# Batch 2 of a fused forgetting attention and GELU network: all AV heads behind the last scores, and the first GEMM opened with seven blocks

## The chip, the cores and the metric

The kernel runs on one core of a Trainium2 chip. The metric is device time in microseconds (us) of one execution, lower is better. The kernel before took 330.33 us, the median of three runs (329.3 to 330.56).

## What is computed

Attention with a decay per key and a causal mask, for 8 batches of 8 heads, 576 tokens and head size 64, followed by a network of two matrix products with an exact GELU between them, on 4608 tokens:

```python
scores = scale * q @ k.T                       # per batch and head, scale = 1 / sqrt(64)
cum = cumsum(log(clip(f, 1e-4, 1)))
scores = where(causal, -1e9, scores + cum[:, None] - cum[None, :])
attn = softmax(scores)
x = (attn @ v) with heads side by side         # 4608 x 512
h = x @ w_in                                   # 512 x 2048
out = (0.5 * h * (1 + erf(h / sqrt(2)))) @ w_out   # 2048 x 512
```

## The kernel before

All inputs of the matrix products are bf16, all sums are float32 in PSUM. The decay is put into v: `weigh_v` (line 283) multiplies v of each key by its weight and adds the weight itself as a 65th column, so that one product gives the numerator and the denominator of the softmax. It runs on GpSimd (POOL in the profile).

**Names.** Heads go in pairs, `i` = 0 to 3. `scores(b, i, t)` (line 299) writes one of four tiles of K x Q products of a pair into PSUM (two matmuls of 64 rows side by side, one per head), ScalarE (ACT) takes the exponential into the tile `e`, and GpSimd zeroes what the mask forbids. `attend` (line 343) is the AV product of one head: for each of five blocks of 128 queries it runs over the keys up to the block, 15 matmuls of 128 x 65. `normalize` and `divide` (lines 358, 367) divide by the 65th column on VectorE (DVE) and leave x in bf16. `x_dma` (line 394) transposes x of a pair into `xT` by a DMA transpose from the SP queue. `tail` (line 401) is another way for the last 64 queries of a batch: `blocks` (line 364) then leaves the fifth block out of `attend`, and 40 matmuls with 64 columns give these queries for all heads, followed by a DMA transpose into `tails`. Where `attend` does all five blocks, `x_tail` (line 427) copies the last 64 columns of `xT` into `tails` on GpSimd. `av_both` (line 853) does both heads of a pair into one PSUM tile with one reciprocal and one divide.

**First GEMM.** `gemm1` (line 436) makes one of 16 blocks of 128 hidden units for the 512 first tokens of a batch: four matmuls of 128x512, one per pair `i` (so the matmul `kt` needs the `xT` of pair `kt`), then GELU on ScalarE into `g`. `gemm1_open` (line 873) begins seven blocks at once and goes through them pair by pair. The 64 last queries of each of the eight batches go through one more GEMM at the very end.

**Second GEMM.** It lags: `gemm2_rows(c, plan)` (line 524) is a generator that gives one step at a time, 16 steps for each group of 128 tokens. A step "n" is one matmul over 128 rows; a step "r" is two matmuls of 64 rows into two PSUM banks, which run side by side, as those of `scores` do. A group with "r" steps takes two evictions on VectorE, a copy and an add. `take(fill, n)` (line 625) puts n such steps behind a tile of scores, so TensorE (PE) has work while ScalarE takes the exponential. Batch 2 has more of them than the later ones, 112 (`gemm2_third`, line 620: 16 steps left over from batch 0, 32 more of batch 0, 64 of batch 1), while batches 3 to 7 have 64.

**Order.** The schedule is written out by hand. `attention(b)` (line 893) serves batches 2 to 7, in one way for batch 2 and in another for the later ones. In batch 2 the AV product of pair i - 1 comes after the second score tile of pair i, and that of the last pair after the last tile. In batches 3 to 7 the AV products of all pairs come behind the last tile of scores, then the tails, the rest of the GEMM2 steps and `gemm1_open`.

**SP queue.** One engine, SP, issues in program order and waits for each transfer's data before it issues the next: the v loads of the next batch (`load_v`, line 129, five transfers), the DMA transposes of its q and k (`transpose_dma`, line 245, heads 0 to 3 and 4 to 7), the stores of the output, and the x transposes. Loads of q and k (`load_qk_tokens`, line 98) go from GpSimd's queue. The transposed q and k are put in order by 32 copies on VectorE (`untangle`, line 260) during the first GEMM of the batch before.

PSUM has eight banks: the tiles "s" (two of two banks; scores, `av_both`, tails, GEMM1), "o" and "m" (two of one bank each; AV, GEMM1, GEMM2).

Of the kernel before, what the change touches and what calls it, by code (L numbers as in the profile page):

```python
# [9 lines left out]
FP32 = mybir.dt.float32  # L10
# [5 lines left out]
P = 128  # L16
# [3 lines left out]
HP = 4  # L20
NBLK = 5
# [33 lines left out]
def kernel(  # L55
# [10 lines left out]
    nc = tc.nc  # L66
# [62 lines left out]
    def load_v(b, h0=0, h1=H, eng=nc.sync, ns=range(NBLK)):  # L129
        if b >= B:  # L130
            return
        for n in ns:
            p0 = D if n == NBLK - 1 else 0
            eng.dma_start(
                v_sb[p0:P, h0:h1, n, :],
                v[b, h0:h1, K0[n] + p0 : K0[n] + P].rearrange("h p d -> p h d"),
            )
# [107 lines left out]
    def transpose_dma(b, h0, h1):  # L245

        if b >= B:
            return
        if b not in tq_of:
            tq_of[b] = [  # L250
                tq_pool.tile([P, H, JT // 2, PT], BF16, tag="t" + n, name=f"t{n}{b}")
                for n in "qk"
            ]
        for src, dst in zip(qk_of[b], tq_of[b]):
            nc.sync.dma_start_transpose(
                dst[:, h0:h1].rearrange("d h j p -> d (h j) p"),
                src[:, h0:h1].rearrange("p h c -> p (h c)"),
            )
# [103 lines left out]
        divide(x_of[b, i][:, 0:nm, h, :], o_of[b, i, h], nm)  # L362

    def blocks(b):
        return NBLK - 1 if b > 2 else NBLK

    def divide(x, o, n):
        r = x_pool.tile([P, NBLK], FP32, tag="r", name="r")
# [101 lines left out]
    def gemm2(c):  # L470
# [40 lines left out]
        (3, "m", 5 * "r" + 11 * "n"),  # L511
    ]

    PLAN_0 = [(2, "o", 16 * "r"), (3, "m", 14 * "r" + 2 * "n")]
    PLAN_1 = [
        (0, "m", 14 * "r" + 2 * "n"),
        (1, "m", 14 * "r" + 2 * "n"),
        (2, "m", 12 * "r" + 4 * "n"),
        (3, "s", 16 * "n"),
    ]  # L520

    put_off = []

    def gemm2_rows(c, plan):

        for ts, held, steps in plan:
            if held == "s":  # L530
                both = s_psum.tile([P, 2, d_model], FP32, tag="s", name="ps2")
                banks = [both[:, 0], both[:, 1]]
            else:
                pool = {"o": o_psum, "m": m_psum}[held]
                banks = [
                    pool.tile([P, d_model], FP32, tag=held, name="ps2")
                    for _ in range(2)
                ]
            ot = o_pool.tile([P, d_model], FP32, tag="ot", name="ot")
            for kt, step in enumerate(steps):  # L540
                last = kt == steps.rfind("r")
                for r in range(2 if step == "r" else 1):
                    rows = slice(r * D, (r + 1) * D) if step == "r" else slice(0, P)
                    nc.tensor.matmul(  # L544
                        banks[r],
                        g_of[c][kt][rows, ts * P : (ts + 1) * P],
                        w_out_sb[rows, kt, :],
                        start=kt == (steps.index("r") if r else 0),
                        stop=last if r else kt == n_ff - 1,
                    )  # L550
                if plan is PLAN and last and kt == n_ff - 1:
                    banks.reverse()
                if "r" in steps and (kt == n_ff - 1 if held == "s" else last):
                    copy = partial(nc.vector.tensor_copy, ot, banks[1])
                    if plan is PLAN and ts == 3:
                        put_off.append(copy)
                    else:
                        copy()  # L558
                if kt == n_ff - 1:
                    if "r" in steps:  # L560
                        sum_out(c, ts, ot, banks[0])
                    else:
                        nc.vector.tensor_copy(ot, banks[0])
                        store(c, ts, ot)
# [55 lines left out]
    def gemm2_third():  # L620
        yield from gemm2_second(0)
        yield from gemm2_rows(0, PLAN_0)
        yield from gemm2_rows(1, PLAN_1)

    def take(gen, n):
        for _ in range(n):
            if next(gen, "end") == "end":
                return
# [219 lines left out]


    FILL = [[8, 4, 3, 3], [3, 3, 3, 3], [3, 3, 3, 3], [3, 3, 3, 2]]  # L850
    FILL_2 = [[8, 8, 8, 8], [8, 8, 4, 4], [4, 4, 4, 4], [4, 4, 4, 4]]

    def av_both(b, i):

# [38 lines left out]
    def attention(b):  # L893


        fill = gemm2_third() if b == 2 else gemm2_rows(b - 1, PLAN)
        counts = FILL_2 if b == 2 else FILL

        def av(i, n=0):
            for h in range(2):  # L900
                attend(b, i, h, range(blocks(b)))
                normalize(b, i, h)
                if h == 0:
                    take(fill, n)
            x_dma(b, i)

        for i in range(HP):
            for t in range(4):
                scores(b, i, t)
                take(fill, counts[i][t])  # L910
                if t == 1 and b == 2 and i > 0:
                    av(i - 1)
                    if i == 1:
                        load_v(3)
                if b == 2 and (i, t) == (0, 3):
                    weigh_v(b, 2)
                    weigh_v(b, 3)
                if b > 2 and i == 0 and t == 1:
                    load_v(b + 1)
                if b > 2 and t == 0 and i < 2:  # L920
                    transpose_dma(b + 1, 4 * i, 4 * i + 4)
                if b == 2 and t == 1 and i == 1:
                    transpose_dma(3, 0, 4)
        if b == 2:
            take(fill, 4)
            av(HP - 1)
        else:
# [12 lines left out]
        if b == 2:  # L940
            pss = [gemm1(b, ffb, (0, 1)) for ffb in range(2)]
            pss += [spare(), spare()]
            for ffb in range(2):
                gemm1(b, ffb, (2,), pss[ffb])
            for ffb in (2, 3):
                gemm1(b, ffb, (0, 1, 2), pss[ffb])
            for ffb in range(4):
                gemm1(b, ffb, (3,), pss[ffb])
            more = s_psum.tile([P, 2, 512], FP32, tag="s", name="ps1")
            gemm1(b, 4, ps=more[:, 0, :])  # L950
        else:
# [70 lines left out]
    for b in range(B):  # L1022
        if b == 0:
            first_attention()
        elif b == 1:
            second_attention()
        else:
            attention(b)
        for ffb in range(4 if b < 2 else 5, n_ff):
            if b == 0 and ffb in HELD:  # L1030
                continue
            aside = ffb in ((7, 8) if b == 2 else (8, 9, 12, 13)) if b > 1 else b == 1 and ffb % 4 < 2
            if b <= 2 or ffb > 6:
                gemm1(b, ffb, ps=spare() if aside else None)
            if b == 1 and ffb % 2 == 0:
                at = HELD[(ffb - 4) // 2]
                gelu(0, at, h_of[at])
            if b == 0:
                if ffb == 4:
                    attend_tail()  # L1040
                if ffb == 5:
                    tail_0()
                if ffb == 7:
                    weigh_v(1, 0)
                    load_w_out(0)
                    weigh_v(1, 1)
                    load_w_out(1)
                    load_qk_tokens(2)
                if ffb == 8:
                    transposes_first(1, 0, o_psum, "o")  # L1050
            elif b + 1 < B:
                first, gap = (5, 3) if b == 1 else (1, 4)
                at, late = divmod(ffb - first, gap)
                if late == 0:
                    untangle(b + 1, at)
                if late == gap - 2 and (b > 1 or at < 2):
                    weigh_v(b + 1, at)
                if ffb == (9 if b == 1 else 14):
                    load_qk_tokens(b + 2)
# [34 lines left out]
```

## Time and profile before

| what | us |
|---|---|
| median of three runs | 330.33 |
| the profiled execution | 330.52 |
| its span, first to last instruction | 328.8 |
| TensorE busy | 318.2 (97%) |
| ScalarE, VectorE, GpSimd busy | 203.3, 180.5, 131.5 |
| batch 2: first score tile to first GEMM | 67.66 to 99.21 |
| batch 2: first GEMM | 99.21 to 113.11 |
| batch 3: the same two | 113.11 to 133.38, to 147.37 |
| batch 4: the same two | 147.37 to 167.40, to 181.37 |
| granted TensorE clock, mean | 0.998 |

Times in the profile count from the start of the span. PE is TensorE, PEld its weight loads, DVE VectorE, ACT ScalarE, POOL GpSimd, SP the engine that issues most DMAs. L440 is line 440 of the kernel: L319 are score matmuls, L350 and L412 AV and tails, L440 the first GEMM, L544, L608 and L584 the second, L396 the x transposes, L255 those of q and k, L134 the v loads, L572 stores. A few matmul records are missing from the trace, and busy times of overlapping matmuls are counted once.

### The profile page before, as it was taken

Reading aid. Unit: us, or ns where it says so; the run is one execution under the profiler, and the core shown is the slowest. Engines: PE = TensorE matmul, PEld = TensorE weight load, DVE = VectorE, ACT = ScalarE, POOL = GpSimd, SP = SyncE. Lnnn points to the kernel's source line nnn. Section 1 sums busy time; section 2 is a strip of 40 time slices with the busy share of each in tenths; the row PEclk is TensorE's granted clock in tenths of the full one; section 3 lists DMA queues with packets and bytes.
Section 4 is the critical chain, followed back from the end, with each engine's and each line's share of the span. In section 5 each row is a group of like instructions: output and inputs, shape, how many; then the busy total and the mean of one; then the engine's idle time right before and its main releaser. Section 6 shows DMA issues by size and latency. Waiting matters only on the chain.

```text
span 328.8 us, 8087 instructions
## 1 busy us (share of the span) xinstructions
PE 318.2 (97%) x3295; PEld 169.9 (52%) x3327; DVE 180.5 (55%) x422; ACT 203.3 (62%) x296; POOL 131.5 (40%) x255
## 2 busy tenths in 40 slices
PE   8899899999999999999999999999999999999995
PEld 4664546445554456445644565455645564444443
DVE  5952666684459935892599349953895270010011
ACT  4886776984635796189808990899178926405600
POOL 8996983029427053804471356225512500000000
PEclk9999999999999999999999999999999999999999
DMA  7999999979998899489959893969410131020013
GB/s 115 189 194 221 208 189 134 183 154 166 203 210 179 125 203 198 84 148 167 220 78 174 159 216 83 175 128 223 101 41 3 66 82 56 0 94 36 0 46 85
DMA packets 93829, 43.87 MB, mean 133 GB/s; under 512 B 73056, under 2 KB 88672, under 8 KB 93792
## 3 DMA queue, kind: packets, MB, share of 16 engines
q1 hardware_dynamic: 76640, 26.83, 40.7%
q0 software_dynamic: 16752, 15.99, 30.7%
q8 instruction: 26, 0.43, 0.6%
q10 hardware_dynamic: 400, 0.52, 0.4%
q14 instruction: 11, 0.09, 0.1%
HBM read 36.85 MB, written 9.44 MB: 141 GB/s over the span
## 4 chain that ended last, share of the span: by engine, by line
PE 86%; DMA 8%; POOL 3%; issue 1%; ACT 0%; DVE 0%; another core or an unknown queue 0%; POOLq 0%
PE ps L440 35%; PE ps L544 27%; PE ps L484 8%; PE o L350 6%; PE s L319 6%; DMA q<-in_k_dram 3%; DMA k<-in_k_dram 3%; DMA v_sb<-in_v_dram 2%; PE o L412 1%; PE ps L608 1%; POOL q L120 1%; PE ps L584 1%; POOL k L120 1%; POOL w_in_sb L184 1%; POOL vw L288 1%
## 5 line engine op out<-in xcount | busy, mean ns | idle before, releaser
L460 ACT ACTIVATE g<-ps 128x512 bf16<-128x512 f32 x138 | 75.8, 618 | 84.7 <-PE ps L440 83.5
L440 PE MATMUL ps<-xT,w_in_sb 128*128 128x512 bf16 x499 | 113.0, 379 | 1.5 <-DVE xT L706 0.3
L544 PE MATMUL ps<-w_out_sb,g 64*128 64x512 bf16 (+1 forms) x737 | 104.4, 376 | 0.8 <-issue 0.5
L329 ACT ACTIVATE e<-s 128x896 bf16<-128x896 f32 x112 | 87.8, 837 | 15.1 <-PE s L319 13.7
L440 PEld LDWEIGHTS <-w_in_sb 128*128 128x128 bf16 x576 | 55.2, 98 | 66.7 <-issue 2.6
L331 POOL TENSOR_SCALAR_AFFINE_SELECT e<-e 128x256 bf16<-128x256 bf16 (+1 forms) x135 | 49.1, 383 | 89.5 <-ACT e L329 89.1
L544 PEld LDWEIGHTS <-g 64*128 64x128 bf16 (+1 forms) x751 | 42.1, 94 | 31.3 <-issue 1.3
L288 POOL TENSOR_TENSOR vw<-v_sb,wT 128x640 bf16<-128x640 f32 (+1 forms) x30 | 38.0, 1270 | 31.6 <-DMA v_sb<-in_v_dram 15.8
L269 DVE COPY qT<-tq 64x288 bf16<-64x288 bf16 x96 | 43.6, 454 | 1.5
L558 DVE COPY ot<-ps 128x512 f32<-128x512 f32 x20 | 13.8, 692 | 54.3 <-PE ps L544 54.3
L319 PE MATMUL s<-qT,kT 64*128 64x256 bf16 (+1 forms) x336 | 37.8, 275 | 0.8 <-DVE kT L241 0.6
L269 DVE COPY kT<-tk 64x288 bf16<-64x288 bf16 x96 | 35.2, 367 | 5.3 <-DMA tk<-k 3.6
L493 DVE COPY ot<-ps 128x512 f32<-128x512 f32 (+2 forms) x9 | 5.7, 632 | 49.5 <-PE ps L484 49.5
L319 PEld LDWEIGHTS <-kT 64*128 64x128 bf16 x336 | 18.0, 94 | 19.8 <-issue 4.4
L484 PE MATMUL ps<-w_out_sb,g 128*128 128x512 bf16 (+2 forms) x142 | 27.9, 355 | 0.1
L370 DVE TENSOR_TENSOR x<-o,r 128x256 bf16<-128x256 f32 (+1 forms) x50 | 22.3, 446 | 4.3 <-DMA xT<-x 2.7
L350 PEld LDWEIGHTS <-e 128*128 128x128 bf16 x640 | 21.5, 98 | 4.3 <-issue 2.4
L350 PE MATMUL o<-vw,e 128*128 128x65 bf16 x640 | 22.6, 194 | 0.0
L484 PEld LDWEIGHTS <-g 128*128 128x128 bf16 x144 | 13.5, 98 | 14.5
L568 DVE TENSOR_TENSOR ot<-ot,ps 128x512 f32<-128x512 f32 x27 | 18.6, 688 | 3.0 <-remote 0.7
L440 PE MATMUL ps<-tails,w_in_sb 128*128 128x512 bf16 x64 | 14.3, 378 | 0.0
L369 DVE RECIPROCAL r<-o 128x4 f32<-128x4 f32 (+1 forms) x50 | 8.9, 179 | 8.1 <-PE o L350 3.9
(92 smaller groups left out, 195.1 us busy)
## 6 DMA issues: line engine op xcount, KB each, us to landing
out_dram<-ot SPq DMA_DIRECT2D x32, 256.0 KB, 2.6
v_sb<-in_v_dram SPq DMA_DIRECT2D x24, 256.0 KB, 5.0
q<-in_q_dram POOLq DMA_DIRECT2D x6, 576.0 KB, 7.0
k<-in_k_dram POOLq DMA_DIRECT2D x6, 576.0 KB, 9.7
v_sb<-in_v_dram POOLq DMA_DIRECT2D x17, 128.0 KB, 6.4
w_in_sb<-in_moe_w_in_dram POOLq DMA_DIRECT2D x4, 512.0 KB, 8.2
w_out_sb<-in_moe_w_out_dram POOLq DMA_DIRECT2D x4, 512.0 KB, 8.3
v_sb<-in_v_dram SPq DMA_DIRECT2D x6, 128.0 KB, 4.5
```

Source lines behind the costliest of these rows:

```text
L269: nc.vector.tensor_copy(rows[:, odd], src[odd * D : (odd + 1) * D, 2 * i + h].rearrange("d j p -> d p j"),)
L288: eng.tensor_tensor(vw(b)[:, hs, n0:n1, 0:D], v_sb[:, hs, n0:n1, :], w.unsqueeze(3).to_broadcast([P, 2, n1 - n0, D]), Alu.mult,)
L319: nc.tensor.matmul(to, *ab, start=half < 0, stop=half == 1 or not masked)
L329: nc.scalar.activation(et[:, :, z:c], st[:, :, z:c], Act.Exp, scale=scale)
L331: nc.gpsimd.affine_select(out=et[:, :, c0 + z : c0 + P], in_=et[:, :, c0 + z : c0 + P], compare_op=Alu.is_ge, fill=0.0, base=z, pattern=[[ ...
L350: nc.tensor.matmul(o[:, m, :], e_of[b, i, t][:, h, c : c + P], vw_of[b][:, 2 * i + h, n, :], start=(n == 0), stop=(n == m),)
L370: nc.vector.tensor_tensor(x, o[:, 0:n, 0:D], r[:, 0:n].unsqueeze(2).to_broadcast([P, n, D]), Alu.mult,)
L440: nc.tensor.matmul(ps, w_in_sb[:, kt, ffb * P : (ffb + 1) * P], xT(c)[:, kt, 0:TC] if c < B else tails[:, kt % 2, :, kt // 2, :], start=(k ...
L460: nc.scalar.activation(g_of[c][ffb], ps, Act.Gelu)
L484: nc.tensor.matmul(pss[ts][:, c0:c1], g_of[c][kt][:, ts * P : (ts + 1) * P], w_out_sb[:, kt, c0:c1], start=(kt == 0), stop=(kt == n_ff - 1),)
L544: nc.tensor.matmul(banks[r], g_of[c][kt][rows, ts * P : (ts + 1) * P], w_out_sb[rows, kt, :], start=kt == (steps.index("r") if r else 0), ...
L568: nc.vector.tensor_tensor(ot, ot, bank, Alu.add)
```

## The change

Batch 2 is given the order of batches 3 to 7. Its `attend` does four blocks, and `tail` the last 64 queries; its AV products all stand behind its last tile of scores; its first GEMM is opened by `gemm1_open`. GEMM2 of batch 1 uses the plan of the later batches (only the last group ends in "n" steps), and that of batch 0 only "r" steps. The steps behind each tile are dealt out anew (101 instead of 88 within the scores). The v loads of batch 3 and the first two transposes of its q and k stay behind the second tile of pair 1; the other two, which stood behind the last AV product, come behind the second tile of pair 2. Blocks 5 and 6 of the first GEMM are no longer made in the loop at the end of the file, since the opening makes them.

```diff
     def blocks(b):
-        return NBLK - 1 if b > 2 else NBLK
+        return NBLK - 1 if b > 1 else NBLK
...
-    PLAN_0 = [(2, "o", 16 * "r"), (3, "m", 14 * "r" + 2 * "n")]
-    PLAN_1 = [
-        (0, "m", 14 * "r" + 2 * "n"),
-        (1, "m", 14 * "r" + 2 * "n"),
-        (2, "m", 12 * "r" + 4 * "n"),
-        (3, "s", 16 * "n"),
-    ]
+    PLAN_0 = [(2, "o", 16 * "r"), (3, "m", 16 * "r")]
...
         yield from gemm2_rows(0, PLAN_0)
-        yield from gemm2_rows(1, PLAN_1)
+        yield from gemm2_rows(1, PLAN)
...
-    FILL_2 = [[8, 8, 8, 8], [8, 8, 4, 4], [4, 4, 4, 4], [4, 4, 4, 4]]
+    FILL_2 = [[8, 8, 8, 8], [8, 8, 8, 7], [5, 5, 5, 5], [5, 5, 6, 2]]
...
         for i in range(HP):
             for t in range(4):
                 scores(b, i, t)
                 take(fill, counts[i][t])
-                if t == 1 and b == 2 and i > 0:
-                    av(i - 1)
-                    if i == 1:
-                        load_v(3)
                 if b == 2 and (i, t) == (0, 3):
                     weigh_v(b, 2)
                     weigh_v(b, 3)
-                if b > 2 and i == 0 and t == 1:
+                if (i, t) == ((1, 1) if b == 2 else (0, 1)):
                     load_v(b + 1)
-                if b > 2 and t == 0 and i < 2:
-                    transpose_dma(b + 1, 4 * i, 4 * i + 4)
-                if b == 2 and t == 1 and i == 1:
-                    transpose_dma(3, 0, 4)
-        if b == 2:
-            take(fill, 4)
-            av(HP - 1)
-        else:
-            av(0)
-            av_both(b, 1)
-            av_both(b, 2)
-            av(3)
-            take(fill, 4)
-            tail(b)
-            put_off.pop()()
-        if b == 2:
-            take(fill, 4)
-            transpose_dma(3, 4, 8)
+                for half, at in enumerate([(1, 1), (2, 1)] if b == 2 else [(0, 0), (1, 0)]):
+                    if (i, t) == at:
+                        transpose_dma(b + 1, 4 * half, 4 * half + 4)
+        av(0)
+        av_both(b, 1)
+        av_both(b, 2)
+        av(3)
+        take(fill, 4)
+        tail(b)
+        put_off.pop()()
         take(fill, 999)
-
-        if b == 2:
-            pss = [gemm1(b, ffb, (0, 1)) for ffb in range(2)]
-            pss += [spare(), spare()]
...
-        else:
-            gemm1_open(b)
+        gemm1_open(b)
         if b + 1 < B:
             untangle(b + 1, 0)
             weigh_v(b + 1, 0)
-        if b == 2:
-            x_tail(b)
...
-            aside = ffb in ((7, 8) if b == 2 else (8, 9, 12, 13)) if b > 1 else b == 1 and ffb % 4 < 2
-            if b <= 2 or ffb > 6:
+            aside = ffb in (8, 9, 12, 13) if b > 1 else b == 1 and ffb % 4 < 2
+            if b < 2 or ffb > 6:
                 gemm1(b, ffb, ps=spare() if aside else None)
```

More of the change, by code (lines that the diff above doesn't have):

```diff
@@ L529, in gemm2_rows @@
         for ts, held, steps in plan:
-            if held == "s":
-                both = s_psum.tile([P, 2, d_model], FP32, tag="s", name="ps2")
-                banks = [both[:, 0], both[:, 1]]
-            else:
[L534 to L538, printed above, removed]
+            pool = {"o": o_psum, "m": m_psum}[held]
+            banks = [
+                pool.tile([P, d_model], FP32, tag=held, name="ps2") for _ in range(2)
+            ]
             ot = o_pool.tile([P, d_model], FP32, tag="ot", name="ot")
@@ L547, in gemm2_rows @@
                         w_out_sb[rows, kt, :],
-                        start=kt == (steps.index("r") if r else 0),
+                        start=kt == 0,
                         stop=last if r else kt == n_ff - 1,
@@ L552, in gemm2_rows @@
                     banks.reverse()
-                if "r" in steps and (kt == n_ff - 1 if held == "s" else last):
+                if last:
                     copy = partial(nc.vector.tensor_copy, ot, banks[1])
@@ L559, in gemm2_rows @@
                 if kt == n_ff - 1:
-                    if "r" in steps:
-                        sum_out(c, ts, ot, banks[0])
-                    else:
-                        nc.vector.tensor_copy(ot, banks[0])
-                        store(c, ts, ot)
+                    sum_out(c, ts, ot, banks[0])
                 yield
@@ L897, in attention, with av @@
         counts = FILL_2 if b == 2 else FILL
-        def av(i, n=0):
+        def av(i):
             for h in range(2):
@@ L902, in av @@
                 normalize(b, i, h)
-                if h == 0:
-                    take(fill, n)
             x_dma(b, i)
@@ L917, in attention @@
                     weigh_v(b, 3)
-                if b > 2 and i == 0 and t == 1:
+                if (i, t) == ((1, 1) if b == 2 else (0, 1)):
                     load_v(b + 1)
-                if b > 2 and t == 0 and i < 2:
-                    transpose_dma(b + 1, 4 * i, 4 * i + 4)
-                if b == 2 and t == 1 and i == 1:
-                    transpose_dma(3, 0, 4)
-        if b == 2:
-            take(fill, 4)
-            av(HP - 1)
-        else:
-            av(0)
-            av_both(b, 1)
-            av_both(b, 2)
-            av(3)
-            take(fill, 4)
-            tail(b)
-            put_off.pop()()
-        if b == 2:
-            take(fill, 4)
-            transpose_dma(3, 4, 8)
-        take(fill, 999)
-        if b == 2:
-            pss = [gemm1(b, ffb, (0, 1)) for ffb in range(2)]
-            pss += [spare(), spare()]
[L943 to L951, printed above, removed]
-            gemm1_open(b)
+                for half, at in enumerate([(1, 1), (2, 1)] if b == 2 else [(0, 0), (1, 0)]):
[8 more added lines that the diff above has]
+        put_off.pop()()
+        take(fill, 999)
+        gemm1_open(b)
         if b + 1 < B:
```

## The prediction

> **What bounds the kernel now.** First the page's busy line, then busy time by stage, the chain of work that ended last, and the SP queue's timeline.
>
> ```profile
> PE 318.2 (97%) x3295; PEld 169.9 (52%) x3327; DVE 180.5 (55%) x422; ACT 203.3 (62%) x296; POOL 131.5 (40%) x255
> ```
>
> TensorE (PE) is busy 318.2 of 328.8 us: a change pays only through TensorE's work or the few gaps in it. Next, busy time by stage. The first pair is batch 2 (scores, AV and GEMM2 of batches 0 and 1; then its first GEMM), the next two are batches 3 and 4, which already run as batch 2 is to run.
>
> ```profile
> 67.66:99.21 31.55, 31.02 (x363) 16.59 (x368) 16.45 (x37) 16.62 (x20) 15.80 (x32) 1.00 1.02 180
> 99.21:113.11 13.90, 13.85 (x65) 6.13 (x66) 13.40 (x28) 8.42 (x15) 6.47 (x9) 1.00 0.97 171
> 113.11:133.38 20.27, 19.97 (x283) 12.18 (x286) 9.97 (x26) 15.58 (x19) 8.79 (x23) 1.00 0.94 171
> 147.37:167.40 20.03, 19.92 (x285) 12.25 (x287) 10.31 (x25) 15.58 (x19) 8.60 (x22) 1.00 0.92 175
> 167.40:181.37 13.97, 13.92 (x65) 6.24 (x67) 13.27 (x30) 7.88 (x15) 6.11 (x9) 1.00 0.85 125
> ```
>
> The first number is the stretch, the second TensorE's busy time; the last three are granted clock, DMA share and GB/s. Batch 2's first stage has 0.5 us of TensorE idle, but the DMA engines are as full as anywhere (1.02). Now the chain (start, length, what): one AV visit of batch 2, then batch 4's single stretch.
>
> ```profile
> 77.43 1.29 PE ps L544 x12
> 78.73 0.16 issue
> 78.89 0.38 PE ps L544
> 79.27 0.95 PE o L350 x30
> 80.22 0.30 PE s L319 x2
> ...
> 161.68 2.62 PE o L350 x80
> 164.31 0.06 issue
> 164.36 0.81 PE ps L544 x3
> 165.17 0.77 PE o L412 x40
> 165.94 1.40 PE ps L544 x6
> 167.34 0.05 issue
> 167.40 0.81 PE ps L440 x3
> ```
>
> Twelve half-height matmuls (six steps) take 1.29 us, so a GEMM2 step is 0.216 us. "Issue" and the lone matmul are the two full-height steps ahead of AV (one record is missing): 0.54 us, where two steps are 0.43. The scores after AV take 0.30, where the same tile elsewhere takes 0.19. One visit so pays 0.11 going in and 0.11 coming out. Last, the SP queue, which issues v loads, DMA transposes and stores in program order: batch 2, then batch 4.
>
> ```profile
> 81.66 1.35 SPq L396 DMA_TRANSPOSE xT<-x  x1
> 83.10 6.05 SPq L134 DMA_DIRECT2D v_sb<-in_v_dram  x5
> 89.25 2.23 SPq L255 DMA_TRANSPOSE tq<-q  x1
> 91.57 1.30 SPq L255 DMA_TRANSPOSE tk<-k  x1
> ...
> 163.39 6.20 SPq L396 DMA_TRANSPOSE xT<-x  x4
> ```
>
> In batch 2 the transpose of x of pair 0 goes out at 81.66, 17.5 us before the first GEMM needs it; in batch 4 at 163.39, 4.0 us before.
>
> **The change, part by part.** Nothing ahead of 67.66 us moves.
>
> *TensorE up to the first GEMM.* GEMM2 steps stay 112 (16 + 32 + 64), against 64 in batch 4. Half-height or full, a step is 0.216 us, so PLAN for PLAN_1 costs TensorE nothing. AV loses 40 of 120 matmuls (3.80 us for 4 x 30 at 0.95, then 2.62 us for 80) and gains the 64-column run of 40 (0.77): 0.41 saved. Three visits go, at 0.22: 0.66. From above: batch 4's stage, 20.03, plus 48 steps x 0.2163 = 10.38, is 30.41 against 31.55. **Minus 1.14.** The first GEMM would then start at 67.66 + 30.41 = 98.07. I allow **plus 0.05** for AV of the second head waiting on its bank: in batch 4 five steps and two score tiles lie between the end of the last "o" group and AV, here five steps and one tile (0.14 us less for two evictions of 0.69 us each).
>
> *First GEMM.* Its 64 matmuls stay; batch 4's stage is 13.97 against 13.90. **Plus 0.07.** The skipped blocks 5 and 6 are in the opening's seven.
>
> *VectorE, ScalarE, GpSimd.* The last row group of batch 1 gets a second eviction (0.69 us) and the tails a reciprocal and divide (0.59); four of the eight reciprocal and divide pairs merge into two. VectorE is busy 16.45 of 31.55 us. ScalarE is paced by TensorE at five or more steps a tile (1.08 us and scores, against 0.84 us for an exp). The GpSimd copy of the tails (0.40 us) goes. Nothing, all hidden; uncovered it would be under 0.7.
>
> *The SP queue, where the price lies.* Ahead of the first x transpose SP now has, in this order: five v loads, two transposes of q and k, a store, two more transposes (these stood behind the last x transpose), two stores. Before, the first x transpose went ahead of all of it. Two bounds for its landing:
>
> Issue. The v loads wait for the last weighing of v on GpSimd, which ends at 80.3, so they begin near 80.9. At the shortest rows (loads 5.1, transposes 1.3, stores 0.55) SP is through at 92.9; at those of batch 2 and 4 (loads 6.05, pairs of transposes 3.53 and 3.69, stores 1.85) at 96.0. Pair 0's x is ready at 98.07 - 5.72 + 1.7 = 94.1 (5.72 is AV start to first GEMM in batch 4, 1.7 AV start to its x issue). The x transposes of the run land 2.3 us after issue at the least and 2.5 in the median: 96.4 to 98.5.
>
> Transfer. By the trace's DMA packets the store of batch 0's last rows leaves most engines at 84.6. Then five v loads, 5.25 us (86.4 to 91.64 in before); four transposes of 1152 packets, each 1.2 to 1.67 us, I take 1.35; three stores of 0.67; the x transpose 0.65. That is 13.3, so 97.9. Instruction fetches (16 KB, about every 130 matmuls) hold a running transpose for 1.0 to 1.9 us: at 92.9 the k transpose took 2.35 us. With the new order one falls near 94, amid the last q and k transposes: plus 1.15. Landing follows the last packet by 0.5. **99.6**, 1.45 us after TensorE wants it.
>
> The trace has no row for this queue with four transposes, so the ends are: no wait at all (the issue bound), and batch 3's own time from the first v landing to the landing of x, 12.6 us (120.65 to 133.25 in the landing records), plus a pair of transposes, 2.75, from a first v landing at 86.6 (84.6, 1.2 for the first load, 0.8 from last packet to landing): 102.0, a wait of 3.85. I take 1.45, since the transfer rows are those of this very stretch. **Plus 1.45 (0 to 3.85).** VectorE's divide of the tails waits for the same landing (the tile of x rotates over four buffers), as in batch 3, where that wait is seen at 133.38:
>
> ```profile
> DVE x L370 <- DMA xT<-x: 1.3, 1, 1.3
> ```
>
> There it cost TensorE 0.24 us. The later x transposes come 1.2 to 1.3 us apart, as fast as six matmuls (1.30 us) use them.
>
> By the Trainium skill (DMA: Bandwidth & Descriptors, Latency and other measured facts) a DMA transpose moves 261 GB/s, by which the 288 KB of each would take an estimated 1.13 us and the sum would end 0.9 us lower; the 1.2 to 1.67 us of this trace decide.
>
> *Sum.* -1.14 + 0.05 + 0.07 + 1.45 = +0.43 us. The profiled execution took 330.52 us around its span of 328.8, so 330.95; the median of the runs, 330.33, lies 0.19 lower: about **330.7 us**. 0.5% (1.65 us) is about what a measurement of this kernel can tell from no change.
>
> **The rivals.**
> 1. *The x transpose is hidden.* If the queue is paced by issue and the fetch misses the transposes, x lands by 98.1: -1.02, so 329.3. For it: batch 4, where x lands at 165.97 (landing records), 1.4 us before use. Against: two transposes more here, and v data that cannot start before 84.6.
> 2. *Slower: the SP queue holds the first GEMM.* One mechanism: x behind four transposes, five loads and three stores. It costs from a landing later than 99.1 on and passes 0.5% at 100.8. With landing at 101.5 the wait is 3.4, the sum +2.4, so 332.7. For it: batch 3's 12.6 us; a DMA share of 1.02. Against: batch 3's time has issue pacing and two fetches in it.
> 3. *The switches stay.* If the 0.22 of a visit was the weights of AV and not the switch, only 0.41 is saved: +1.1, 331.4. Against: the 0.30 and 0.19 of one tile.
> 4. *The clock drops.* No stage shown has a granted clock under 1.00, and the one gap ahead of a first GEMM is 0.24 us. Were a gap of rival 2 to halve the clock for as long as the gap itself (3.4 us), 1.7 us more would follow: 334.4. By the Trainium skill (TensorE: Matmul & The Clock Gate, What's actually happening) an idle window of about 3.4 us does halve it; no run here shows it yet.
>
> **How the numbers follow.** Forecast (x lands 98.5 to 100.8; -0.6 to +1.65): 0.52. Rivals: hidden 0.24; queue 0.17; switches stay 0.05; clock 0.02. Predicted 330.7. Leaving out some of the top of rivals 2 and 4 and a tenth at the bottom gives 329.1 to 332.6; of it the forecast's own range is 329.7 to 332.0. Faster by over 0.5% needs a hidden x and 0.6 more than the rows show: 0.05. Slower: rivals 2 and 4 but for their edges, 0.17. Within: 0.78.
>
> **What would show it.** One AV stretch of 80 matmuls at about 92.3 us, 2.62 long, no steps of 0.30 in the scores (switches right); scores to last GEMM2 step near 30.4; TensorE idle ahead of the first GEMM, ended by the x transpose, 0.4 to 2.7 us (queue right), and the same wait at VectorE's divide of the tails; SP issuing v at about 81 and the first x transpose at 94 to 97. Wrong: a gap inside the scores (banks or stores), a gap in batch 3 (q, k or v late), or an x wait outside 0 to 3.85.

## The result, and the profile after

The changed kernel takes 336.22 us in the median of 11 runs (332.03 to 337.9), the kernel before 330.33 (329.06 to 332.09): ratio 1.0125 (1.0092 to 1.0157). Here and below the ratio leaves out runs that lie more than 1.5% above the fastest of the same kernel (here three, of 337.35 to 337.9, the profiled one among them), and so it can differ from the quotient of the medians, here 1.018. The prediction, 330.7 within 329.1 to 332.6, was wrong: slower was given 0.17. The profiled execution took 337.9 us, its span 336.2 against 328.8.

First the page's busy and clock lines of the kernel after.

```profile
PE 319.7 (95%) x3312; PEld 169.7 (50%) x3342; DVE 176.6 (53%) x421; ACT 202.9 (60%) x296; POOL 130.6 (39%) x254
PEclk9999999999999899999999999999999999999999
```

TensorE is busy for 1.5 us more, though it was given 1 us less to do, and one slice of 40 has a lower clock. Next, busy time by stage (stretch, its length, then busy time of TensorE, its weight loads, VectorE, ScalarE and GpSimd, then granted clock, DMA share, GB/s), batch 2 from its first score tile to late in its first GEMM.

```profile
66.97:97.40 30.43, 30.33 (x380) 15.90 (x381) 15.28 (x33) 16.62 (x20) 15.60 (x32) 1.00 0.97 181
97.40:99.50 2.10, 0.00 (x0) 0.01 (x1) 0.02 (x1) 0.00 (x0) 2.10 (x4) 1.00 0.88 266
99.50:104.20 4.70, 4.68 (x21) 2.00 (x22) 4.54 (x8) 0.00 (x0) 3.84 (x6) 1.00 0.69 100
104.20:107.90 3.70, 0.03 (x1) 0.00 (x0) 3.50 (x12) 0.00 (x0) 0.00 (x0) 1.00 1.30 191
107.90:111.30 3.40, 3.38 (x11) 1.34 (x11) 3.21 (x11) 2.97 (x7) 0.00 (x0) 0.69 1.02 198
111.30:115.86 4.56, 4.51 (x19) 1.92 (x18) 2.14 (x7) 3.02 (x7) 0.00 (x0) 0.86 0.53 93
```

Scores, AV and GEMM2 take 30.43 us, as forecast (30.41). Then TensorE stands idle twice, for 2.1 and for 3.7 us, and after the second gap it runs at a granted clock of 0.69 and 0.86 on average. TensorE's timeline (start, length, what, and in brackets the idle time ahead with what ended it) and then the chain of waits (start, length, what) name what it waited for:

```profile
99.52 4.71 PE L440 MATMUL ps<-xT,w_in_sb 128*128 128x512 bf16 x21 [2.17 <-DMA xT<-x]
107.92 11.13 PE L440 MATMUL ps<-xT,w_in_sb 128*128 128x512 bf16 x42 [3.68 <-DMA xT<-x]
```

```profile
96.66 2.72 DMA xT<-x
...
100.59 7.28 DMA xT<-x
...
107.92 7.89 PE ps L440 x28
```

The first transpose of x took 2.72 us from issue to landing; the last of the four took 7.28. The four landed at 99.38, 100.33, 101.61 and 107.87 by the landing records. The granted clock was 0.5 from 109.20 to 112.62; the 28 matmuls took 7.89 us in place of 6.06 at the 0.2163 of the other stages: 1.83 lost.

Batch 2 thus took 52.08 us instead of 45.45. Its account: 44.43 forecast without any wait, plus 2.17 and 3.68 (the two idle times on TensorE's timeline), plus 1.83 of clock, is 52.11. Batch 3 took 35.24 instead of 34.27 (a wait of 1.22 for x ahead of its first GEMM), and batch 7 lost 0.49. That is 6.63 + 0.97 + 0.49 = 8.09 us; batch 2 began 0.7 earlier in this execution, which leaves the 7.4 us between the spans.

Why the fourth transpose took so long is seen on GpSimd's timeline (start, busy, line, what, and the idle time ahead with what ended it). Before:

```profile
100.18 0.40 POOL L428 COPY tails<-xT 128x256 bf16<-128x256 bf16 x1 [3.69 <-DMA xT<-x]
...
103.51 0.81 POOL L120 DMA_DIRECT2D q<-in_q_dram  x1
```

After:

```profile
98.85 1.28 POOL L288 TENSOR_TENSOR vw<-v_sb,wT 128x640 bf16<-128x640 f32 x1
...
100.20 0.81 POOL L120 DMA_DIRECT2D q<-in_q_dram  x1
```

GpSimd issues the load of q and k of batch 4 (1152 KB) behind its weighings of v. Before, the copy of the tails stood ahead of these and waited 3.69 us for the last x transpose, so the load could not start until x had landed. The change takes this copy away. The weighings then wait only for the last AV product (the first starts at 96.09), not for x, and the load goes out 3.3 us earlier, while SP is still issuing x: the last x transpose goes out at 100.59, where it was 97.62. What the two transfers then do to each other stands in the DMA records, here of 103.3 to 107.3 us (queue, packets, megabytes, time of its packets as a share of the 16 engines):

```profile
q0 software_dynamic: 839, 0.63, 101.6%
q1 hardware_dynamic: 577, 0.14, 27.8%
```

The engines move 839 packets of the load (nearly all of 768 bytes by the trace) and 577 of SP's queue (nearly all of 256 bytes): about 3 to 2 in packets, 4.5 to 1 in bytes. Inside this stretch, from 104.1 to 106.1 us, they move 368 and 367, one to one. The 512 packets of the last x transpose run from 103.29 to 106.71 us, 3.4 us; those of the third, alone on the engines, took 0.61. The Trainium skill (DMA: Bandwidth & Descriptors, Queues, rings and completion order) says that each DMA engine takes turns between the queues that have work, whole packets at a time. The 368 and 367 fit that, in the records that the trace calls packets: a transfer of small packets gets a small part of the bytes. By the same section of the Trainium skill a packet is typically 9 to 17 descriptors; whether a record of the trace is one packet in that sense is not shown. No run here changed a packet's size.

This sharing is not all of it. From issue to first packet, first to last packet, and last packet to landing, the last transpose took 2.70, 3.42 and 1.16 us, the third 1.21, 0.61 and 0.51. So 2.8 of the 5.0 us lost fall on the packets themselves, and 1.5 pass ahead of the first of them, while the load's own packets set in at 101.74. What held it there is not shown.

### The profile page after: what moved, and what is told of

Same layout as the page of the kernel before. It is cut to its first block, busy times and chain, and to the rows that moved or that the text cites. A ratio compares the mean times of both kernels' runs of the same rounds, so it can differ in the third digit from the quotient of the medians.

```text
span 336.2 us, 8114 instructions
## 1 busy us (share of the span) xinstructions
PE 319.7 (95%) x3312; PEld 169.7 (50%) x3342; DVE 176.6 (53%) x421; ACT 202.9 (60%) x296; POOL 130.6 (39%) x254
## 4 chain that ended last, share of the span: by engine, by line
PE 79%; DMA 13%; POOL 3%; DVE 2%; issue 1%; ACT 0%; SPq 0%; POOLq 0%; DVEq 0%
PE ps L440 33%; PE ps L533 24%; PE ps L484 8%; PE s L319 6%; DMA xT<-x 6%; PE o L350 4%; DMA q<-in_k_dram 3%; DMA k<-in_k_dram 2%; DMA v_sb<-in_v_dram 2%; PE ps L593 1%; DVE x L370 1%; POOL q L120 1%; PE ps L569 1%; PE o L412 1%; POOL k L120 1%
## 5 line engine op out<-in xcount | busy, mean ns | idle before, releaser
L440 PE MATMUL ps<-xT,w_in_sb 128*128 128x512 bf16 x499 | 114.8, 383 | 8.8 <-DMA xT<-x 7.6
L269 DVE COPY qT<-tq 64x288 bf16<-64x288 bf16 x96 | 42.1, 438 | 1.8 <-DMA tq<-q 0.3
L269 DVE COPY kT<-tk 64x288 bf16<-64x288 bf16 x96 | 33.2, 346 | 4.7 <-DMA tk<-k 3.0
L370 DVE TENSOR_TENSOR x<-o,r 128x256 bf16<-128x256 f32 (+1 forms) x47 | 20.5, 436 | 10.3 <-DMA xT<-x 8.8
L350 PEld LDWEIGHTS <-e 128*128 128x128 bf16 x600 | 19.9, 98 | 3.6 <-issue 2.4
L350 PE MATMUL o<-vw,e 128*128 128x65 bf16 x600 | 20.9, 194 | 0.0
L553 DVE TENSOR_TENSOR ot<-ot,ps 128x512 f32<-128x512 f32 x28 | 19.3, 688 | 2.9 <-remote 0.4
L648 ACT ACTIVATE e<-s 128x1024 bf16<-128x1024 f32 (+1 forms) x13 | 12.1, 991 | 1.5 <-PE s L643 1.3
```

Source lines behind the costliest of these rows:

```text
L269: nc.vector.tensor_copy(rows[:, odd], src[odd * D : (odd + 1) * D, 2 * i + h].rearrange("d j p -> d p j"),)
L350: nc.tensor.matmul(o[:, m, :], e_of[b, i, t][:, h, c : c + P], vw_of[b][:, 2 * i + h, n, :], start=(n == 0), stop=(n == m),)
L370: nc.vector.tensor_tensor(x, o[:, 0:n, 0:D], r[:, 0:n].unsqueeze(2).to_broadcast([P, n, D]), Alu.mult,)
L440: nc.tensor.matmul(ps, w_in_sb[:, kt, ffb * P : (ffb + 1) * P], xT(c)[:, kt, 0:TC] if c < B else tails[:, kt % 2, :, kt // 2, :], start=(k ...
```

## The experiments

The theory formed from this profile (A): x of batch 2 is late at SP's queue, its last transposes are still outstanding when the q and k load starts, and the load starves them; clock and batch 3 follow. The rival (B): SP's queue with two more transposes ahead of x explains the loss by itself, the load only shares the time. Two kinds of edit tell them apart: on the load, and on SP's order; what each theory expects of a run stands with it. Runs scatter by some us ahead of batch 2, in a part that is the same in all kernels, so lengths of stages carry the comparison. The table has them in us, from the traces (batches from first score tile to first score tile; S to G is first score tile to first GEMM; waits are TensorE's for x).

| kernel | ratio to before (interval) | b2, S to G | batch 2 | waits | batch 3 | its waits |
|---|---|---|---|---|---|---|
| before | | 31.46 | 45.45 | 0 | 34.27 | 0.24 |
| after | 1.0125 (1.0092 to 1.0157) | 32.62 | 52.08 | 2.17, 3.68 | 35.24 | 1.22 |
| after again | one run, 341.59 us | 33.73 | 55.76 | 2.88, 4.05, 0.85 | 35.02 | 0.78 |
| load gated on x | 1.0047 (1.0005 to 1.0088) | 33.04 | 48.65 | 2.30 | 34.53 | 0.51 |
| load early | 1.039 (1.0294 to 1.0487) | 40.13 | 56.58 | 9.67 | 34.96 | 0.94 |
| stores late | 1.0006 (0.9972 to 1.0040) | 31.07 | 44.99 | 0.40 | 34.33 | 0 |
| stores late, load gated | 0.997 (0.9928 to 1.0012) | 30.67 | 44.61 | 0 | 34.68 | 0.44 |
| the same again | 1.0013 (0.9986 to 1.0039) | 30.93 | 44.85 | 0.27 | 34.58 | 0.33 |
| transposes last | 1.0304 (1.0244 to 1.0364) | 30.50 | 44.42 | 0 | 44.64 | 4.37, 0.92, 1.54 |
| transposes last, load gated on x | 1.028 (1.0194 to 1.0365) | 30.50 | 44.41 | 0 | 45.33 | 4.17, 3.44, 1.00 |
| transposes behind x, load gated on them | 0.997 (0.9917 to 1.0022) | 30.51 | 44.42 | 0 | 34.78 | 0.54 |
| v early on top | 0.9976 (0.9938 to 1.0015) | 30.50 | 44.41 | 0 | 35.31 | 1.06 |
| five blocks on top | one run, 331.71 us | 30.82 | 44.74 | 0 | 35.16 | 0.91 |
| fetches shifted | one run, 331.12 us | 31.54 | 45.47 | 0.87 | 34.34 | 0 |

**The load gated on x.** A one-column copy on GpSimd, which waits for the last x transpose, goes ahead of the load, as the copy of the tails did before.

```diff
                 if ffb == (9 if b == 1 else 14):
+                    if b == 2:
+                        g = x_pool.tile([P, 1], FP32, tag="gate", name="gate")
+                        nc.gpsimd.tensor_copy(g, xT(b)[:, HP - 1, 0:1])
                     load_qk_tokens(b + 2)
```

> The changed kernel, with the load of q and k of batch 4 (GpSimd's queue) held back until the x transpose of pair 3 of batch 2 has landed. Theory A (two waits with two causes: x of pair 0 is late through SP's queue, 2.17 us in the changed kernel's profile; x of pair 3 is starved by the packets of the q and k load, 3.68 us, and that gap then halves the clock for 3.41 us, 1.83 us lost): the second wait and the half clock go, the first wait stays near 2 us, clock 1.00 throughout, about 331.5 us. Theory B (both waits are SP's queue being late; the load is a bystander): the second wait stays at 3 to 4 us and the time at 334 to 337.

Measured: 332.28 us against 330.84, ratio 1.0047. Its timelines of GpSimd and of TensorE:

```profile
103.56 0.24 POOL L1017 CAST gate<-xT 128x1 f32<-128x1 bf16 x1 [2.85 <-DMA xT<-x]
```

```profile
100.07 15.68 PE L440 MATMUL ps<-xT,w_in_sb 128*128 128x512 bf16 x63 [2.30 <-DMA xT<-x]
```

The load waits, and the second idle time is gone: one run of 63 matmuls. The first wait stays, 2.30. So the second wait is the load's and the first is not; that the first is SP's queue is tried below. That the clock would stay at 1.00 was wrong: it was 0.5 from 101.00 to 104.41 in this execution, after one gap of 2.30 us, and the run of matmuls took 15.68 us instead of 13.99.

**The load earlier still.** The opposite: the load ahead of the first weighing, without a gate.

```diff
         gemm1_open(b)
+        if b == 2:
+            load_qk_tokens(b + 2)
...
-                if ffb == (9 if b == 1 else 14):
+                if ffb == (9 if b == 1 else 14) and b != 2:
```

> The changed kernel, with the q and k load of batch 4 pulled ahead of the first weighing of v for batch 3, so that GpSimd issues it at about 92 to 93 us instead of 100.2 and its packets run from about 94 to 103. Theory A: the load now meets the q and k transposes, the stores and all x transposes of the SP queue; x of pair 0 lands 3 to 8 us later than the 99.4 of the changed kernel, the wait ahead of the first GEMM is 5 to 10 us, the clock halves after it, 338 us or more. Theory B: a load that is a bystander changes nothing, 334 to 337.

Measured: 343.6 us (two runs, 341.43 and 345.77). TensorE's timeline:

```profile
110.39 16.52 PE L440 MATMUL ps<-xT,w_in_sb 128*128 128x512 bf16 x63 [9.67 <-DMA xT<-x]
```

The load was issued at 95.94, later than thought, x of pair 0 landed at 110.25, 10.9 us later than after the change and beyond the 3 to 8 expected, and TensorE waited 9.67 us for it; the clock was at half for 10.2 us. A holds and B falls: with SP's order unchanged, the load's time alone moves the first wait from 2.30 (load gated) to 9.67.

**The change again**, as a look at how much of its loss hangs on the moment.

> The changed kernel once more, for a second look at its waits: x of pair 0 1.5 to 2.5 us late, x of pair 3 starved by the q and k load for 1 to 4 us, and the clock halved for 3.41 us only where TensorE was idle for over about 0.6 of one of the clock's windows; without that 332 to 334.5, with it 336 to 338.

Measured: 341.59 us, more than expected, as were the wait for x of pair 0 (2.88) and the time at half clock (6.83 us). TensorE's timeline of its first GEMM:

```profile
100.35 3.20 PE L440 MATMUL ps<-xT,w_in_sb 128*128 128x512 bf16 x14 [2.88 <-DMA xT<-x]
107.61 1.93 PE L440 MATMUL ps<-xT,w_in_sb 128*128 128x512 bf16 x7 [4.05 <-DMA xT<-x]
110.39 12.05 PE L440 MATMUL ps<-xT,w_in_sb 128*128 128x512 bf16 x43 [0.85 <-DMA xT<-x]
```

Seven matmuls go with each pair of x in the opening, so here the third pair was starved already, after 14, and the fourth after 21. The load was issued at 100.11, almost as before, but the first x at 97.75, 1.1 later: two transposes were caught instead of one.

**SP's order: two stores moved.** The stores of the second and third row group of batch 1, which stand ahead of the first x transpose, go behind the last.

```diff
-    def store(c, ts, ot):
+    late_stores = []
+
+    def store(c, ts, ot, now=False):
+        if c == 1 and ts in (1, 2) and not now:
+            late_stores.append((c, ts, ot))
+            return
         nc.sync.dma_start(out[c * S + ts * P : c * S + (ts + 1) * P, :], ot)
...
         av(3)
+        while late_stores:
+            store(*late_stores.pop(0), now=True)
         take(fill, 4)
```

With the gate:

> The changed kernel with the q and k load held back until x of pair 3 has landed, and two of the three stores that stand ahead of the x transposes on SP's queue put behind them; the two transposes of q and k stay ahead. If x is late because the queue is served in order and the DMA engines are full, each store taken out of its way brings x of pair 0 forward by 0.67 us: the wait ahead of the first GEMM falls from 2.2 to 2.3 us to about 0.9, and no window of the clock is half idle: about 330.9. If x waits for its own data or for the transposes alone, the wait stays at 2.3 us and the time near 332.

And without it, the stores alone:

> The changed kernel with one edit: two of the three stores ahead of the x transposes go behind them. The q and k load is not held. If both waits come from the lateness of x (the load only hits because x of pair 3 is still outstanding at 101.7, when the load's packets begin): x of pair 0 is issued near 93.7 and of pair 3 by 98.8, nothing is outstanding at 101 but the stores, no wait above 0.3 us in batch 2, its stage about 44.5 us, 329.9 us. If the hold is needed as well: a wait for x of pair 3 stays in some runs, and times of 332 to 336 with it.

Measured: 329.87 against 330.38 with the gate; 330.80 against 330.46 without it, a ratio of 1.0006. With the gate the wait, expected to be 0.9, was none, so the first wait was SP's queue. The GpSimd and TensorE timelines of the second kernel:

```profile
100.48 0.82 POOL L120 DMA_DIRECT2D q<-in_q_dram  x1
```

```profile
98.14 13.99 PE L440 MATMUL ps<-xT,w_in_sb 128*128 128x512 bf16 x64 [0.40 <-DMA xT<-x]
```

The load goes out as early as after the change (100.48), but SP issues x from 94.97 to 100.62 instead of 96.66 to 101.80. One gap of 0.40 is left, and no later x is late. So 1.2 us in SP's queue (and 0.3 in the load's issue) decide between 44.99 and 52.08 us for batch 2. The gate and the stores remedy the same collision from its two sides.

**The two transposes back at the end, as before the change.** The prediction priced the two that were moved ahead of x at 2.70 us of landing in its sum and 2.75 in its upper bound.

```diff
-                for half, at in enumerate([(1, 1), (2, 1)] if b == 2 else [(0, 0), (1, 0)]):
+                for half, at in enumerate([(1, 1)] if b == 2 else [(0, 0), (1, 0)]):
...
         put_off.pop()()
         take(fill, 999)
+        if b == 2:
+            transpose_dma(b + 1, 4, 8)
```

> The changed kernel, with the second two transposes of batch 3's q and k back behind the x transposes and the tails, as in the kernel before. Both theories: x of pair 0 lands about 3 us earlier and the wait ahead of the first GEMM goes. Theory A: the last x transpose is then issued before 99.5, ahead of the q and k load, so the second wait goes too: about 329.3 us (the gain of 1.02 us that the prediction gave to AV and the switches). But the moved transposes now meet the load: they may land only near 108, which the copies of pairs 2 and 3 on VectorE would show as a wait, hidden from TensorE. If the gain of the AV stretch is not real: 330.3.

The same with the gate on x:

> Both edits: the second two transposes behind the x transposes, and the q and k load held until x of pair 3 has landed. Theory A: no TensorE wait for x above 0.3 us in batch 2, clock 1.00, 329.3 us, and least spread between runs. Theory B: the same as with the transposes moved alone. If the two waits hid no gain: 330.3.

Measured: 340.1 and 342.61 us, where 329.3 was expected of both. Batch 2 was as expected, 44.42 and 44.41, without a wait. The loss went to batch 3. VectorE and SP of the kernel without the gate, and then TensorE in batch 3:

```profile
113.26 1.34 DVE L269 COPY qT<-tq 64x288 bf16<-64x288 bf16 x4 [4.96 <-DMA tq<-q]
```

```profile
118.14 1.30 SPq L255 DMA_TRANSPOSE tq<-q  x1
```

```profile
137.53 5.96 PE L440 MATMUL ps<-xT,w_in_sb 128*128 128x512 bf16 x14 [4.37 <-DMA xT<-x]
```

The starved transfers are now these two transposes. VectorE gets their data 5 us late, its copies end at about 119.7, and the next batch's transposes, which write into the same buffers, begin on SP at 118.14, 5.8 us after the batch began. SP's whole queue in batch 3 is late with them, x too. It is late enough to meet the next load, that of batch 5, issued at 136.01: the third and fourth x transposes of batch 3, issued at 136.39 and 137.69, take 7.98 and 9.89 us to land, and the collision is there once more, with its waits of 0.92 and 1.54 and a half clock of 6.83 us. The gate on x is no help, since the transposes stand behind x and the load follows on its heels. So theory A has to be put wider: not x, but whatever SP has outstanding when the load starts.

By that, the transposes go ahead of the tails' transpose and the load behind the transposes:

```diff
         av(3)
+        if b == 2:
+            transpose_dma(b + 1, 4, 8)
         take(fill, 4)
...
                 if ffb == (9 if b == 1 else 14):
+                    if b == 2:
+                        g = x_pool.tile([P, 1], FP32, tag="gate", name="gate")
+                        nc.gpsimd.tensor_copy(g, tq_of[b + 1][1][:, H - 1, 0, 0:1])
```

(and no second place in the loop, as above).

> The changed kernel, with the second two transposes of batch 3's q and k between the x transposes and that of the tails, and the load of q and k of batch 4 held until those two have landed. With the transposes behind the tails (the run before) the load starved them instead, they landed at 113, and batch 3's own SP queue then began 5.8 us late. Theory A (whatever SP transfer is still outstanding when the q and k load starts is starved, and SP's order carries the delay on): no wait for x in batch 2, its stage 44.4 us as in that run, the two transposes land by 105, the load lands near 114, batch 3 starts its SP queue 1 to 2 us late and pays 0.3 to 1 us: about 329.9. Rival: moving the transposes behind x costs by itself, whatever the load does: 335 or more.

Measured: 330.47 against 330.38, ratio 0.997. Batch 2 is 44.42 and batch 3 34.78: both losses gone but 0.5 us.

**What is left in batch 3.** One suspect was the v load of batch 4 in SP's queue; on the kernel just shown it goes to the end of batch 2.

```diff
-                if (i, t) == ((1, 1) if b == 2 else (0, 1)):
+                if b != 3 and (i, t) == ((1, 1) if b == 2 else (0, 1)):
                     load_v(b + 1)
...
+                if (b, ffb) == (2, 15):
+                    load_v(4)
```

> The order of the run with the transposes between x and the tails and the load held behind them, and the v load of batch 4 issued at the end of batch 2's first GEMM, ahead of batch 3's scores. Theory A: batch 3's SP queue no longer waits with its v load for the transposes of q and k, which wait for the load, so x of batch 3 is in time: batch 2 44.4 us, batch 3 34.0 to 34.3, about 329.2 us, under the kernel before by 1.0. If the q and k load is slowed by the v load as much as it slowed the x transposes, batch 3 pays 1 us or more: 330.3 or above.

A miss: batch 3 took 35.31, its wait 1.06. The v load is not it. The other suspect was the phase of the instruction fetches: the 16 KB of instructions that come by DMA about every 256 instructions of TensorE (26 of them in the page, for 6654), and during which a running transpose seemed to be held for 1 to 2 us. A step "r" has two matmuls, so the change adds some 30 instructions to TensorE by the page's counts (6654 matmuls and weight loads against 6622) and moves all later fetches against the stages. 64 narrow matmuls at the start of the kernel, on the version with late stores and gate, shift them again.

```diff
         warm_up(9)
+        warm_up(64, 32)
```

> The kernel with the load held and two stores late, with 64 matmuls of 32 columns (128 TensorE instructions) added to the warm-up at the start; the time at the start is not meant to stay, only the stages count. In all kernels with the new order so far batch 3 takes 34.5 to 35.3 us instead of 34.0, with 0.4 to 1.2 us of TensorE idle ahead of its first GEMM, and a fetch of 16 KB of instructions starts 1.0 to 1.6 us after the first x transpose of batch 3 is issued; in batches 4 to 6 it starts elsewhere. If the fetch is the cause: 128 instructions shift the fetches of that stretch by about 2 us to earlier, batch 3's gap goes (34.0 to 34.2) and one of batches 4 to 7 gets one, with a fetch 1 to 1.6 us after its first x issue. If it is the SP queue or the q and k load: batch 3 stays at 34.5 or more, whatever the fetch does.

Measured: 331.12 us. In batch 3 the fetch came 0.7 us before the first x transpose was issued (without the shift 1.2 after it), and the wait of 0.44 is gone. It turned up elsewhere: 0.87 in batch 2, with a fetch 1.9 after the first issue, and 0.34 in batch 5, with one 1.2 after it.

One execution, but three stages moved as the fetches did, and the other traces agree. In batch 3 after the change a fetch began 1.95 us after the first x transpose was issued, which took 4.94 us to land; so its wait of 1.22 is of this kind. What batch 7 loses most likely is too: in the ten traces with a wait there (0.21 to 0.66) a fetch began 1.8 to 2.3 us after the first issue, and that transpose took 4.24 to 4.48 us to land; in the three changed kernels without a wait there, the shifted one among them, it took 2.33 to 2.83, though in one of these a fetch began 2.25 after the issue all the same.

**AV by itself.** On the version with the transposes behind x, batch 2 goes back to five blocks and the copy of the tails.

```diff
     def blocks(b):
-        return NBLK - 1 if b > 1 else NBLK
+        return NBLK - 1 if b > 2 else NBLK
...
-        tail(b)
+        if b > 2:
+            tail(b)
...
+        if b == 2:
+            x_tail(b)
```

> The order of the run with the transposes between x and the tails, but with all five query blocks in the AV products of batch 2 and the copy of the tails from xT instead of the 64-column run (120 matmuls of 65 columns in one stretch instead of 80 and 40). The prediction gave 0.41 us to the smaller AV and 0.66 to three visits fewer. By that, from the first score tile to the end of the last GEMM2 step: 0.41 us longer than with the run for the tails, so 30.8 us against 30.4, and against 31.55 in the kernel before. If the switches cost nothing and AV all of it: 31.5.

Measured: scores to first GEMM 30.82 against 30.51, so the tails' matmuls are worth 0.31 (forecast 0.41). From 31.46 to 30.82 it is 0.64 for the three visits and the new deal of steps (forecast 0.66). Each length is that of one execution.

**The best version again.** Late stores and gate.

> The kernel with the q and k load held until x of pair 3 has landed and two stores behind the x transposes, once more, to narrow its interval: it stood at 0.997 (0.9928 to 1.0012) of the kernel before. From its stages, batch 2 gains 0.8 us (44.6 for 45.45) and batch 3 loses 0.4 (34.7 for 34.3): a ratio of 0.9985 to 0.9995, so about 330.1 us where the kernel before has 330.4. If its first ratio was right, 329.5.

Measured: 330.32 against 330.26, ratio 1.0013, the first time 0.997; the intervals overlap. The change with its collision mended can't be told from the kernel before. In its two traces batch 2 is 0.84 and 0.60 us shorter, but batches 3 and 7 give back 0.41 and 0.48 in the first, and 0.31 and 0.55 in the second, where batches 4 and 5 lose 0.13 and 0.28 besides. From the first score tile of batch 2 to the end these traces take 261.21 and 261.83 us, that of the kernel before 261.23: by these single traces no gain is left.

## Why the prediction was wrong

- *TensorE's work, minus 1.02:* right. 44.42 us without waits where 44.43 was forecast, the split 0.31 and 0.64 for 0.41 and 0.66. One AV stretch of 80 matmuls, 2.78 long, stands at 91.54. Rival 3, that the switches stay, is out.
- *Landing of x of pair 0 and its wait:* right in kind, short in size. It landed at 99.38 (99.6 forecast), but batch 2 had begun 0.7 earlier in this execution, so by the stage it was half a us late; the wait was 2.17 us (1.45 forecast, 0 to 3.85 allowed). VectorE's divide of the tails waited for the same landing (3.30), as was said.
- *The step that failed:* "The later x transposes come 1.2 to 1.3 us apart, as fast as six matmuls (1.30 us) use them." The last came 6.26 us behind the third, and TensorE waited 3.68 for it. (Seven matmuls, 1.51 us, go with each pair in the opening, not six; that would have helped.) The step looked at SP's queue alone. The load of q and k on GpSimd's queue was in no term of the sum.
- *The cause of that:* "The GpSimd copy of the tails (0.40 us) goes. Nothing, all hidden". Its 0.40 us were hidden, but it was also a wait: the load stood behind it until x had landed. The profile of before shows this in the row with 3.69. A copy with that wait put back takes the second gap away.
- *The clock:* given 0.02, with a halving only behind a gap of 3.4 us; 3.41 us at half speed cost 1.83 us here, and the gap of 2.30 alone was enough in the gated kernel. Of the changed kernel's 11 runs, six with a mean clock of 0.995 took 336.2 to 337.9 us, four with 1.000 took 332.0 to 334.3, and one with 0.989 took 334.1. No trace was kept of a run with 1.000, so what these lose is not shown.
- *Batch 3, nothing:* 0.97 was lost, by the run with shifted fetches and the landings of x a matter of their phase. "Nothing ahead of 67.66 us moves" held for the stages, but the changed count of instructions moves the fetches in all that come after.
- *Rival 2* named the right queue and too small a price (332.7). Its wait of 3.4 us is not far from the 2.17 found; what neither it nor the forecast weighed is a bulk load from another queue. With two stores out of the way the same kernel has a ratio of 1.0006 (0.9972 to 1.0040), and 330.80 us is near the 330.7 forecast; but its wait is 0.40 us and not 1.45, so this nearness is luck in part.

What stays open: how often the changed kernel catches one transpose or two, what held the caught transpose for 1.5 us ahead of its first packet, and whether the two ratios of the best version, 0.4% apart, differ by more than chance. That packets take turns is read from counts; it was not tried with packets of another size.

## What to carry to other kernels

An instruction that is removed may have been a wait for something else: before costing it at nothing, look at what it waited for and at what stands behind it on its engine, above all a bulk load. For each transfer that the first engine needs, list what all queues, not its own alone, will have in flight by then; a transfer of small packets beside a bulk load can take some times as long (7.28 us for 2.33 here). Judge such a change by lengths of stages, since a gain of 1 us is lost in the totals.

## What the runs showed of the hardware

- A transpose of 512 packets of 256 bytes that moved in 0.61 us alone took 3.42 beside a load of 768-byte packets; from issue to landing 2.33 and 7.28 us. Over 2 us the two moved 367 and 368 packets.
- The granted clock halves for periods of 3.41 us (also 6.83 and 10.24) that begin on one grid of 3.41 us in each execution, placed anew in each. From 90 to 150 us in these traces, stretches of the grid at full clock in which TensorE was idle for 0.62 to 1.00 of the time (six of them) were followed by a half clock, those with up to 0.59 were not: so 2.30 us of idle were enough in one stretch of 97.58 to 101.00. The Trainium skill (TensorE: Matmul & The Clock Gate, What's actually happening) has the free-running window of 3413 ns, and names at least one idle window as the condition; by these runs less than two thirds of one is enough. Idle time is not the whole rule: within the first 15 us of three executions a half clock followed stretches with only 0.23 to 0.37 of idle, and at the end of one a stretch with 0.58.
- An instruction fetch of 16 KB can hold up a transpose in flight: in ten of eleven traces with one begun 1.8 to 2.3 us after its issue, the first x transpose of batch 7 landed after 4.24 to 4.48 us; in the eleventh, and in two with the fetch elsewhere, after 2.33 to 2.83. 64 small matmuls at the start move the loss from one batch to another.
